# Clustered attention and two expert layers: reciprocal sums spread by transfers through device memory, additions of output halves one step later

## The chip, the cores and the metric

One program on one core of a Trainium2 chip. The metric is the device time of one execution in microseconds (us), the median over runs. Five engines run in parallel, each in the order of its own instructions: PE (TensorE, matrix products, with its weight loads shown apart as PEld), DVE (VectorE), ACT (ScalarE), POOL (GpSimd) and SP (SyncE), which here issues every transfer. An instruction that needs another engine's result, or a landed transfer, waits for a semaphore at the head of its engine's queue, and everything behind it waits too.

## The reference

Attention over 2 batches, 8 heads, 768 tokens, head width 64, with 16 centroids per head. A query sees only the keys that have the same nearest centroid. Its output is the input of a layer with squared ReLU (512 to 2048 to 512), and that one's output the input of four weighted expert layers.

```
q_assign = argmax(q_n @ c_n)            # nearest centroid, per head
k_assign = argmax(k_n @ c_n)
scores = where(q_assign == k_assign, scale * q @ k^T, -1e9)
attn = exp(scores - rowmax)
attn = attn / (sum(attn) + 1e-9)        # <- the sums whose reciprocals are spread
x    = (attn @ v) as [1536, 512]        # heads side by side
x    = relu(x @ w_in)^2 @ w_out
out  = sum_e p[:, e] * (relu(x @ w1[e]) @ w2[e]),  p = probs / (sum + 1e-9)
```

## The kernel before

Everything is float32; for the products each operand is split into a rounded high part and a low rest (fp32r), and two or three products are added up.

**Attention** takes the first quarter of the time. There are 16 heads (batch times heads), 6 query tiles of 128 rows each, so 96 *steps*, numbered g from 0. Two heads are a *pair* of 12 steps; "step 7" below means g = 7 mod 12, counted from a pair's first step. One step works on four tiles at once: the scores of tile g+2 (`S`, line 590: two products over 128 rows, then two over 80 rows, of which 64 are low parts of q or k and 16 the one-hot rows of the centroid mask), the exponential of tile g+1 (`E`, ACT), the transposes of tile g (`T0`, `T1`, PE, with the copy `pth` on ACT and the rest `ptl` on DVE), and half of the product with v for the pair of tiles before (`P0` or `P1`). `M` is DVE's row maximum for `S`.

The order in which a step's instructions are written is the list `ORDER`, one for even and one for odd steps, and each engine issues in that order. For odd steps it is `S X1 E M T0 T1 Y1 H0 C P1 X2 R L0 H1 C L1 O K Y2 C`. `X1` and `X2` take the next two entries of the step's list `todo`, `Y1` and `Y2` run what these return (their evacuation); entries that are left run after the last letter. `R` runs preparations (`stack`, `hot_rows`, loads), `O` is `emit_PO`, `K` a piece of the conversion of the next layer's first weights (line 189 on ACT and 191 on POOL are its last piece, in step 7 of four pairs), `C` takes one entry of `dq`, a list of small DVE and POOL steps. All four kinds of side work share one PSUM buffer, `ps_m`.

**The one-hot** of the next pair's first head runs beside: maxima on DVE and steps on POOL (lines 456 to 464), then in step 7 `pair_hot` as second entry of `todo`: PE transposes (478), ACT copies to `ohm` (483), and `hot_rows` has SP issue four transfers into the rows 64 to 79 of q2 and k2 (495). The first reader of these rows is `S` of step 10.

**emit_PO** evacuates a finished output of 256 queries. A head's product has a high and a low half in the two halves of the 128 partitions, which must be added. After the pair's first head, at `O` of step 7, SP issues `xm<-xs` (line 666), which moves the low half to the other partitions in the tile xm, of which there is **one buffer** (`bufs=1`); after the second head, at `O` of step 1 of the next pair, two more transfers complete xs and xm (669, 670). At that same `O` the list `nq` gets the eight entries of `norm_slots`, and from step 2 on each step takes one entry of `nq` and appends it to its `todo`.

**norm_slots** is the *norm chain* of a pair; there are seven in the loop (0 to 6; chain 6 falls in the last pair, which prepares no further one-hot and uses no xm), and an eighth after the loop with `last=True`. Step 2, f1: reciprocals of the sums (128 rows x 12) on DVE, split in high and low. Step 6, f2: PE transposes the 24 columns (689), ACT copies them to rt, POOL adds xs and xm in two halves (698). Steps 8 and 9, f3: three products each with the constant selector `sel` (706) spread the 6 rows of each head over its 64 partitions, ACT copies to rb (712), POOL multiplies (713) and splits into the next layer's input (726). Nothing needs that input before the attention ends.

**After the attention** come the squared-ReLU layer and the experts; the change does not touch them.

Of the kernel before, what the change touches and what calls it, by code (L numbers as in the profile page):

```python
# [8 lines left out]
F32 = mybir.dt.float32  # L9
# [3 lines left out]
ALU = mybir.AluOpType  # L13
# [20 lines left out]
def moe_attention_kernel(  # L34
# [171 lines left out]
    with tc.manual_schedule():  # L206
# [7 lines left out]
        pt_p = right(actx, "pt", 2)  # L214
        xs_p = right(actx, "xs", 2)
        sm_p = right(actx, "sm", 4)
        prep = ExitStack()
        nat_p = right(prep, "nat", 1)
        kq_p = right(prep, "kq", 1)
# [32 lines left out]

        def load_direct(i, nm):
            b, h = divmod(i, H)
            x = p_p.tile([128, NTT, D], F32, tag="p", name="p") if i == 0 else (
                xs_p.tile([128, NTT, D], F32, tag="rb", name="rb"))
            a = k if nm == "nk" else q
            nc.sync.dma_start(out=x, in_=a[b, h].rearrange("(p t) d -> p t d", t=NTT))
            nat[i, nm, "raw"] = x
# [409 lines left out]
                    nc.sync.dma_start(out=xs_t[hp][low], in_=xo[low])  # L669
                    nc.sync.dma_start(out=xm_t[hp][low], in_=xo[top])  # L670

        def norm_slots(hp, last=False):
            st = {}
            def f1():
                sm = sums_t.pop(hp)
                r = sm_p.tile([128, 2, NTT], F32, tag="r", name="r", bufs=1)
                rs = st["rs"] = sm_p.tile([128, NTT, 2, 2], F32R, tag="rs", name="rs", bufs=2)
                rv = r.rearrange("p h t -> p t h")
                dq[:0] = [
                    lambda: nc.vector.tensor_scalar(r, sm, 1e-9, None, op0=ALU.add),  # L680
                    lambda: nc.vector.reciprocal(r, r),
                    lambda: nc.vector.tensor_copy(rs[:, :, :, 0], rv),
                    lambda: (nc.vector if last else nc.gpsimd).tensor_tensor(
                        rs[:, :, :, 1], rv, rs[:, :, :, 0].bitcast(F32), op=ALU.subtract),
                ]

            def f2():
                m = ps_m.tile([NTT * 4, 128], F32R, tag="m", name="m")
                nc.tensor.transpose(m, st["rs"].rearrange("p t h s -> p (t h s)"), identr)

                def evac():
                    rt = st["rt"] = xs_p.tile([NTT * 4, 128], F32R, tag="rt", name="rt")
                    nc.scalar.copy(rt, m.bitcast(F32))
                    if hp in xm_t:
                        xm = xm_t.pop(hp)
                        for c0 in range(0, S, HALF):
                            cs = slice(c0, c0 + HALF)
                            nc.gpsimd.tensor_tensor(  # L698
                                xs_t[hp][:, cs], xs_t[hp][:, cs], xm[:, cs], op=ALU.add)
                return evac  # L700

            def f3(half):
                b, kt = divmod(hp, H // 2)
                m = ps_m.tile([128, HALF], F32, tag="m", name="m")
                for j in range(QT):
                    nc.tensor.matmul(  # L706
                        m[:, j * 128:(j + 1) * 128], sel[:, half * QT + j], st["rt"],
                        start=True, stop=True)

                def evac():  # L710
                    rb = xs_p.tile([128, HALF], F32, tag="rb", name="rb")
                    nc.scalar.copy(rb, m)
                    (nc.vector if last else nc.gpsimd).tensor_tensor(
                        rb, rb, xs_t[hp][:, half * HALF:(half + 1) * HALF], op=ALU.mult)
                    c0 = b * S + half * HALF
                    col = c0
                    while col < c0 + HALF:
                        tb, o = divmod(col, TB)
                        n = min(TB - o, c0 + HALF - col)
                        xn = rb[:, col - c0:col - c0 + n]  # L720
                        hi = xh[tb][:, kt, o:o + n]
                        if last:
                            nc.scalar.copy(hi, xn)
                        else:
                            round_pool(hi, xn)
                        (nc.vector if last else nc.gpsimd).tensor_tensor(
                            xl[tb][:, kt, o:o + n], xn, hi.bitcast(F32), op=ALU.subtract)
                        col += n
                return evac

            if last:
                return [f1, f2, lambda: f3(0), lambda: f3(1)]
            return [f1, None, None, None, f2, None, lambda: f3(0), lambda: f3(1)]


        mp = {}
# [368 lines left out]
        for g in range(NU):  # L1105
            par = g % 2
            todo = slots.pop(g, [])
            if nq:
                f = nq.pop(0)
                if f is not None:  # L1110
                    todo.append(f)
            pr, w = divmod(g - 2, 2)
            has_pv = 0 <= pr < NU // 2
            end = {}

            def slot(n):
                if todo:
                    end[n] = todo.pop(0)()

            def T(half):  # L1120
                if g < NU:
                    end["H%d" % half], end["L%d" % half] = emit_T(g, half)

            def PV(half):
                if has_pv and w == half:
                    emit_PV(pr, half)

            def PO():
                if has_pv and w == 1:
                    emit_PO(pr)  # L1130
                    ii, jj = divmod(pr, NTT // 2)
                    if ii % 2 == 1 and jj == NTT // 2 - 1 and pr + 1 < NU // 2:
                        nq.extend(norm_slots(ii // 2))

            def other():
                for f in early.pop(g, []):
                    f()

            def convert():
                if g >= AT["conv"] and cq:  # L1140
                    if not dq and g % (2 * NTT) in AT["turns"]:
                        cq.pop(0)()
                elif not cq and g % NTT == 4:
                    for _ in range(2):
                        lq and lq.pop(0)()

            def finish(n):
                f = end.pop(n, None)
                if f:
                    f()  # L1150

            def products():
                emit_S(g + 2)
                if g == NU - 1:
                    late.append(early_gemm1(0))

            def maximum():
                while late and g < NU - 1:
                    late.pop(0)()
                emit_max(g + 2)  # L1160

            do = {
                "E": lambda: emit_exp(g + 1), "S": products,
                "M": maximum, "P0": lambda: PV(0), "P1": lambda: PV(1),
                "O": PO, "R": other, "T0": lambda: T(0), "T1": lambda: T(1),
                "X1": lambda: slot("Y1"), "X2": lambda: slot("Y2"),
                "C": lambda: dq and dq.pop(0)(),
                "K": convert,
            }
            for a in ORDER[par]:  # L1170
                do[a]() if a in do else finish(a)
            while todo:
                whole(todo.pop(0))
            while late and g == NU - 1:
                late.pop(0)()
            if g == NU - 2:
                prep.close()
                mctx = ExitStack()
                for nm in ("w01", "g", "tp"):
                    mp[nm] = mctx.enter_context(  # L1180
                        tc.tile_pool(name=nm, bufs=1, reuse_waits="tile"))
                w_pool[0, 1] = mp["w01"]
                ga = mp["g"].tile([128, 12 * TB], F32R, name="ga")
                mp["g1"] = ga.rearrange("p (k x t) -> p k x t", k=6, x=2)
                mp["g2"] = ga.rearrange("p (k t) -> p k t", t=HALF)
                fa = mp["tp"].tile([128, 6 * HALF + 1024], F32, name="fa")
                mp["r"] = fa[:, 0:2 * TB].rearrange("p (k t) -> p k t", k=2)
                mp["c"] = fa[:, 0:6 * HALF].rearrange("p (k t) -> p k t", k=6)
                sa = fa[:, 6 * HALF:6 * HALF + 1024]
                mp["s"] = sa.rearrange("p (s k f) -> p s k f", s=4, k=2)  # L1190
                cv_p.append(lambda shp: sa[:, 0:512] if len(shp) == 2 else
                            sa[:, 0:512].rearrange("p (k f) -> p k f", k=shp[1]))


        hp, pr = NH // 2 - 1, NU // 2 - 1
        f1, f2, f3, f4 = norm_slots(hp, last=True)
        f1()
        while dq:
            dq.pop(0)()
# [149 lines left out]
```

## Time and profile before

| | |
|---|---|
| time, median of 3 runs | 1033.24 us (1032.88 to 1033.82) |
| the profiled execution | 1032.07 us, its span 1030.2 us |
| PE busy in the span | 1019.0 us, 99% |
| DVE, ACT, POOL busy | 675.2, 536.3, 568.2 us |
| attention, steps 0 to 95 | up to about 262 us of the span |

The page gives busy times and a chain of waits, followed back from the last instruction: at each step to what released it, or to the instruction before it on its engine. What lies on that chain sets the end. A timeline row is: start, duration of the group, engine, line, operation, tile written <- tiles read, shapes, count, and in brackets how long the engine was idle just before and what ended that. In the chain a piece's duration counts only the time until the next piece takes over, so pipelined products show 0.11 to 0.18 us each there and about 0.3 us in the timeline. SP's queue (SPq) is in the timeline too, with the time that each issue takes.

### The profile page before, as it was taken

What the parts mean: (1) busy time and instruction counts of PE and PEld (TensorE: products, weight loads), DVE (VectorE), ACT (ScalarE), POOL (GpSimd) and SP (SyncE); (2) the same over time, 40 slices, a digit from 0 to 9 for tenths busy, and PEclk for the clock granted to TensorE, in tenths of its full rate; (3) what the DMA queues carried; (4) which work ended last, traced back from release to release, by engine and by line L of the source; (5) the groups of instructions that cost most, each with busy time, mean ns of one, the idle gap of its engine ahead of it and who ended that gap; (6) DMA issues with size and microseconds to landing.
All of it is one profiled execution on the core that took longest, in us unless ns stands there. A gap on an engine that the chain in (4) does not pass through costs nothing.

```text
span 1030.2 us, 14964 instructions
## 1 busy us (share of the span) xinstructions
PE 1019.0 (99%) x5549; PEld 906.1 (88%) x5549; DVE 675.2 (66%) x1054; ACT 536.3 (52%) x1080; POOL 568.2 (55%) x564
## 2 busy tenths in 40 slices
PE   8999999999999999999999999999999999999998
PEld 7999999999888888888888889899888898988887
DVE  8888888889676773731275565577676565555554
ACT  6888889889565433434453333433354333333331
POOL 4567778663332222244456667667678566566550
PEclk9999999999999999999999999999999999999999
DMA  4676656751032320311012112122124122122101
GB/s 120 160 187 143 137 125 162 193 132 46 12 113 84 121 82 13 111 41 41 1 42 82 60 63 82 47 77 82 42 82 143 41 82 81 42 82 68 56 1 61
DMA packets 72456, 86.05 MB, mean 84 GB/s; under 512 B 26944, under 2 KB 49792, under 8 KB 72384
## 3 DMA queue, kind: packets, MB, share of 16 engines
q1 hardware_dynamic: 72384, 85.11, 28.7%
q8 instruction: 43, 0.70, 0.3%
q14 instruction: 29, 0.24, 0.1%
HBM read 59.83 MB, written 3.15 MB: 61 GB/s over the span
## 4 chain that ended last, share of the span: by engine, by line
PE 89%; DVE 5%; POOL 5%; issue 1%; ACT 1%; POOLq 0%; DVEq 0%; ACTq 0%
PE bank L920 25%; PE bank L880 22%; PE bank L773 13%; PE s L590 4%; PE t L623 4%; PE bank L750 4%; PE bank L748 4%; PE bank L749 4%; PE po L637 2%; PE po L639 2%; POOL xs L698 1%; DVE ptl L629 1%; DVE nb L599 1%; PE m L361 1%; PE m L706 1%
## 5 line engine op out<-in xcount | busy, mean ns | idle before, releaser
L920 PE MATMUL bank<-w1h,ga 128*128 128x512 f32 x768 | 269.9, 393 | 0.0
L930 DVE SCALAR_TENSOR_TENSOR x<-bank,pe_p,x 128x512 f32<-128x512 f32 x180 | 134.8, 750 | 167.8 <-PE bank L920 167.7
L880 PE MATMUL bank<-xa,w0h 128*128 128x384 f32 x896 | 228.2, 335 | 0.1
L880 PEld LDWEIGHTS bank<-xa,w0h 128*128 128x128 f32 x896 | 164.5, 188 | 17.9 <-ACT fa L891 0.5
L920 PEld LDWEIGHTS bank<-w1h,ga 128*128 128x128 f32 x768 | 144.1, 188 | 24.5
L759 POOL TENSOR_TENSOR ga<-fa,ga 128x512 fp32r<-128x512 f32 x48 | 63.2, 1317 | 175.4 <-ACT ga L758 134.4
L920 PE MATMUL bank<-w1l,ga 128*128 128x512 f32 x384 | 151.6, 395 | 0.0
L880 PE MATMUL bank<-xa,w0l 128*128 128x384 f32 x448 | 149.7, 334 | 0.0
L891 ACT COPY fa<-bank 128x384 f32<-128x384 f32 x96 | 45.6, 475 | 171.6 <-PE bank L880 171.6
L773 PE MATMUL bank<-ga,w1h 128*128 128x512 f32 x384 | 126.6, 389 | 0.0
L900 ACT ACTIVATE ga<-fa 128x384 fp32r<-128x384 f32 x96 | 50.5, 526 | 135.5 <-DVE fa L894 135.5
L849 POOL TENSOR_TENSOR w0l<-raw,w0h 128x512 fp32r<-128x512 f32 x64 | 75.0, 1194 | 81.2 <-ACT w0h L848 81.2
L867 POOL TENSOR_TENSOR w1l<-raw,w1h 128x1024 fp32r<-128x1024 f32 x32 | 77.3, 2414 | 71.3 <-ACT w1h L866 71.3
L629 DVE TENSOR_TENSOR ptl<-t,pth 128x384 fp32r<-128x384 f32 x192 | 97.9, 549 | 28.3 <-ACT pth L628 27.9
L599 DVE TENSOR_REDUCE nb<-s 128x1 f32<-128x768 f32 x96 | 91.4, 952 | 8.9 <-PE s L590 7.7
L903 DVE SCALAR_TENSOR_TENSOR ga<-fa,ga 128x384 fp32r<-128x384 f32 x96 | 90.1, 939 | 0.6 <-ACT ga L900 0.6
L628 ACT CAST pth<-t 128x384 fp32r<-128x384 f32 x192 | 83.6, 485 | 11.5 <-PE t L623 10.4
L623 PE MATMUL t<-identf,p 128*128 128x128 f32 x576 | 86.9, 275 | 1.6 <-DVE ptl L629 1.5
L610 ACT ACTIVATE p<-s,nb 128x768 f32<-128x768 f32 x96 | 87.5, 911 | 2.0 <-DVE nb L599 1.9
L756 ACT ACTIVATE fa<-bank 128x512 f32<-128x512 f32 x44 | 26.4, 599 | 116.3 <-PE bank L750 116.3
L773 PEld LDWEIGHTS bank<-ga,w1h 128*128 128x128 f32 x384 | 72.1, 188 | 14.7
L590 PE MATMUL s<-k,q 80*128 80x384 f32 (+1 forms) x384 | 84.4, 341 | 0.2 <-DVE q L334 0.2
(209 smaller groups left out, 2066.6 us busy)
## 6 DMA issues: line engine op xcount, KB each, us to landing
raw<-in_moe_w_dram SPq DMA_DIRECT2D x64, 512.0 KB, 4.1
raw<-in_moe_w_in_dram SPq DMA_DIRECT2D x7, 1024.0 KB, 5.1
raw<-in_moe_w_out_dram SPq DMA_DIRECT2D x6, 1024.0 KB, 4.9
k<-nkh SPq DMA_DIRECT2D x28, 192.0 KB, 3.3
q<-nqh SPq DMA_DIRECT2D x28, 192.0 KB, 3.0
nv<-in_v_dram SPq DMA_DIRECT2D x16, 192.0 KB, 3.9
out_dram<-x SPq DMA_DIRECT2D x12, 256.0 KB, 2.1
k<-nkl SPq DMA_DIRECT2D x14, 192.0 KB, 3.8
```

Source lines behind the costliest of these rows:

```text
L590: nc.tensor.matmul(s[:, j, 0:HALF], stk[i, nq][:, t * 128:(t + 1) * 128], stk[i, nk][:, j * HALF:(j + 1) * HALF], start=first, stop=not first)
L599: nc.vector.tensor_reduce(out=nb, in_=s_ps[u][:, :, 0:HALF], axis=AX.XY, op=ALU.max, negate=True)
L610: nc.scalar.activation(p, s_ps.pop(u)[:, :, 0:HALF], AF.Exp, bias=nb_t.pop(u), accum_out=sums_t[hp][:, i % 2, t:t + 1])
L623: nc.tensor.transpose(tp[:, j], p_sb[u][:, half, j * 128:(j + 1) * 128], identf)
L628: return (lambda: nc.scalar.copy(dh, tp), lambda: nc.vector.tensor_tensor(dl, tp, dh.bitcast(F32), op=ALU.subtract))
L629: lambda: nc.vector.tensor_tensor(dl, tp, dh.bitcast(F32), op=ALU.subtract))
L773: nc.tensor.matmul(o, a, b, start=(ft == 0 and z == 0), stop=(ft == NF - 1 and z == 2))
L867: nc.gpsimd.tensor_tensor(lo, w, hi.bitcast(F32), op=ALU.subtract)
L880: nc.tensor.matmul(ps, w[:, o:o + 128], r_op(r, x)[:, kt], start=(first and kt == 0 and z == 0), stop=(kt == 1 and z == 2), skip_group_che ...
L903: nc.vector.scalar_tensor_tensor(out=g_t(n, f, t, 1), in0=h_src(n, f, t), scalar=0.0, in1=g_t(n, f, t, 0).bitcast(F32), op0=ALU.max, op1=A ...
L920: nc.tensor.matmul(o, a, w[:, f], start=(f == 0 and z == 0), stop=(f == 1 and z == 2))
L930: nc.vector.scalar_tensor_tensor(out=acc, in0=o, scalar=pc, in1=acc, op0=ALU.mult, op1=ALU.add)
```

## The change

The norm chain inside the loop becomes `norm_steps`. The reciprocals are no longer split; PE transposes their 12 columns in step 5 instead of 6, ACT copies them, and SP writes the 12 rows of 128 to a tile in device memory. In step 6 SP issues two transfers that read 768 values back into each of 64 partitions (192 KB each). The addition of xs and xm is an entry of its own in step 7, one step later than before: there it is the third entry of `todo`, behind pair_hot, and so runs after the step's last letter (in chain 6 it is the first). Steps 8 and 9 multiply and split on POOL as before, as plain entries. rb is one tile of 768 columns for the whole attention instead of two rotating halves. After the loop `norm_last` does what `norm_slots(last=True)` did, selector products included.

```diff
+        hbm_p = actx.enter_context(tc.tile_pool(name="hbm", bufs=2, space=bass.MemoryType.DRAM))
+        rb_all = xs_p.tile([128, S], F32, tag="rb", name="rb", bufs=1)
...
-        def norm_slots(hp, last=False):
+        def norm_scaled(hp, half, rb, v, hi_copy):
+            b, kt = divmod(hp, H // 2)
+            v.tensor_tensor(rb, rb, xs_t[hp][:, half * HALF:(half + 1) * HALF], op=ALU.mult)
...
+        def norm_steps(hp):
             st = {}
+
+            def f1():
+                sm = sums_t.pop(hp)
+                r = st["r"] = sm_p.tile([128, 2, NTT], F32, tag="r", name="r", bufs=1)
+                dq[:0] = [
+                    lambda: nc.vector.tensor_scalar(r, sm, 1e-9, None, op0=ALU.add),
+                    lambda: nc.vector.reciprocal(r, r),
+                ]
+
+            def f2():
+                m = ps_m.tile([2 * NTT, 128], F32, tag="m", name="m")
+                nc.tensor.transpose(m, st["r"].rearrange("p h t -> p (h t)"), identf)
+
+                def evac():
+                    rt = xs_p.tile([2 * NTT, 128], F32, tag="rt", name="rt")
+                    nc.scalar.copy(rt, m)
+                    rd = st["rd"] = hbm_p.tile([2 * NTT, 128], F32, tag="rd", name="rd")
+                    nc.sync.dma_start(out=rd, in_=rt)
+                return evac
+
+            def f3():
+                rb = st["rb"] = rb_all[:]
+                for h in range(2):
+                    nc.sync.dma_start(
+                        out=rb[h * D:(h + 1) * D],
+                        in_=st["rd"][h * NTT:(h + 1) * NTT].rearrange(
+                            "t n -> (t n)").partition_broadcast(D))
+
+            def f4():
+                xm = xm_t.pop(hp)
+                for c0 in range(0, S, HALF):
+                    cs = slice(c0, c0 + HALF)
+                    nc.gpsimd.tensor_tensor(
+                        xs_t[hp][:, cs], xs_t[hp][:, cs], xm[:, cs], op=ALU.add)
+
+            def f5(half):
+                norm_scaled(hp, half, st["rb"][:, half * HALF:(half + 1) * HALF], nc.gpsimd, round_pool)
+
+            return [f1, None, None, f2, f3, f4, lambda: f5(0), lambda: f5(1)]
+
+        def norm_last(hp):
...
-                    if hp in xm_t:
-                        xm = xm_t.pop(hp)
-                        for c0 in range(0, S, HALF):
-                            cs = slice(c0, c0 + HALF)
-                            nc.gpsimd.tensor_tensor(
-                                xs_t[hp][:, cs], xs_t[hp][:, cs], xm[:, cs], op=ALU.add)
...
-            return [f1, None, None, None, f2, None, lambda: f3(0), lambda: f3(1)]
+            return [f1, f2, lambda: f3(0), lambda: f3(1)]
...
-                        nq.extend(norm_slots(ii // 2))
+                        nq.extend(norm_steps(ii // 2))
```

## Rows read from the trace of the kernel before

**Rows 1.** The page, busy time of the engines.
```profile
PE 1019.0 (99%) x5549; PEld 906.1 (88%) x5549; DVE 675.2 (66%) x1054; ACT 536.3 (52%) x1080; POOL 568.2 (55%) x564
```

**Rows 2.** Windows: busy us (instructions) of PE, PEld, DVE, ACT, POOL; granted clock; DMA; GB/s.
```profile
60.00:260.00 200.00, 196.24 (x1465) 184.32 (x1464) 171.66 (x300) 175.92 (x418) 133.31 (x187) 1.00 0.58 136
```

**Rows 3.** Chain of waits, steps 6 to 10 of chain 2: start, us, what.
```profile
128.16 1.94 POOL xs L698 x2
...
132.05 0.36 POOL oh L464
...
132.46 0.45 PE m L478 x3
132.91 0.78 PE s L590 x4
133.68 0.33 PE t L623 x3
134.01 0.47 PE m L706 x3
134.49 0.48 PE t L623 x3
...
136.38 0.48 PE m L706 x3
136.86 0.80 PE t L623 x6
...
138.38 0.70 PE s L590 x4
```

**Rows 4.** Timeline of PE: transposes of step 5, one-hot transposes of step 7.
```profile
126.16 0.92 PE L623 MATMUL t<-identf,p 128*128 128x128 f32 x6 [0.26 <-DVE ptl L629]
...
132.46 0.45 PE L478 MATMUL m<-identr,oh 128*128 128x128 f32 x3 [0.45 <-POOL oh L464]
```

**Rows 5.** Timeline of SP's queue, chain 2, and last the loads of chain 4.
```profile
125.94 1.34 SPq L243 DMA_DIRECT2D nq<-in_q_dram  x2
...
132.48 0.46 SPq L666 DMA_DIRECT2D xm<-xs  x1
133.45 0.66 SPq L495 DMA_DIRECT2D q<-ohm  x1
134.16 1.28 SPq L495 DMA_DIRECT2D k<-ohm  x2
...
190.97 1.11 SPq L109 DMA_DIRECT2D raw<-in_moe_w_out_dram  x2
```

**Rows 6.** Line 495, the 56 one-hot row transfers.
```profile
DMA to landing us min/median/max: 1.9/2.0/4.2
```

**Rows 7.** Timeline of DVE: the cast of chain 2, the second maximum.
```profile
123.45 0.16 DVE L682 CAST rs<-r 128x12 fp32r<-128x12 f32 x1
...
128.20 0.55 DVE L467 TENSOR_REDUCE mx<-A 128x24 f32<-128x384 f32 x1
```

**Rows 8.** Line 191 on POOL: ns min/median/max, first and last start.
```profile
L191 POOL TENSOR_TENSOR w0l<-cva,w0h x4: 1274/1276/1280, 70.4 to 164.2; 128x512 fp32r<-128x512 f32 x4
```

**Rows 9.** Timeline of POOL: the conversion in step 7.
```profile
133.02 1.27 POOL L191 TENSOR_TENSOR w0l<-cva,w0h 128x512 fp32r<-128x512 f32 x1 [0.61 <-ACT w0h L189]
```

**Rows 10.** Timeline of ACT: the conversion in step 7.
```profile
132.31 0.62 ACT L189 CAST w0h<-cva 128x512 fp32r<-128x512 f32 x1
```

**Rows 11.** Chain of waits: step 10 of chain 4, step 9 of chain 6.
```profile
200.46 0.70 PE s L590 x4
...
255.68 0.49 PE m L706 x3
...
256.25 0.48 ACT rb L712
```

**Rows 12.** DMA issues: count, KB each, median us to landing.
```profile
nq<-in_q_dram SPq DMA_DIRECT2D x12, 192.0 KB, 4.8
```

**Rows 13.** Line 976, the warm-up products at the start: ns min/median/max.
```profile
L976 PE MATMUL po<-identr x41: 278/283/583, 2.0 to 16.7; 128*128 128x256 f32 x41
```

More of the change, by code (lines that the diff above doesn't have):

```diff
@@ L254, in load_direct @@
             b, h = divmod(i, H)
+            o = 0 if nm == "nk" else HALF
             x = p_p.tile([128, NTT, D], F32, tag="p", name="p") if i == 0 else (
-                xs_p.tile([128, NTT, D], F32, tag="rb", name="rb"))
+                rb_all[:, o:o + HALF].rearrange("p (t d) -> p t d", t=NTT))
             a = k if nm == "nk" else q
@@ L670, in emit_PO @@
                     nc.sync.dma_start(out=xm_t[hp][low], in_=xo[top])
-        def norm_slots(hp, last=False):
+        def norm_scaled(hp, half, rb, v, hi_copy):
+            b, kt = divmod(hp, H // 2)
+            v.tensor_tensor(rb, rb, xs_t[hp][:, half * HALF:(half + 1) * HALF], op=ALU.mult)
+            c0 = b * S + half * HALF
+            col = c0
+            while col < c0 + HALF:
+                tb, o = divmod(col, TB)
+                n = min(TB - o, c0 + HALF - col)
+                xn = rb[:, col - c0:col - c0 + n]
+                hi = xh[tb][:, kt, o:o + n]
+                hi_copy(hi, xn)
+                v.tensor_tensor(xl[tb][:, kt, o:o + n], xn, hi.bitcast(F32), op=ALU.subtract)
+                col += n
@@ new lines, in norm_steps @@
+        def norm_steps(hp):
+            st = {}
+            def f1():
[30 more added lines that the diff above has]
+            return [f1, None, None, f2, f3, f4, lambda: f5(0), lambda: f5(1)]
@@ L678, in f1 @@
                 rv = r.rearrange("p h t -> p t h")
[L679 to L685, printed above, removed]
+                V = nc.vector
+                V.tensor_scalar(r, sm, 1e-9, None, op0=ALU.add)
+                V.reciprocal(r, r)
+                V.tensor_copy(rs[:, :, :, 0], rv)
+                V.tensor_tensor(rs[:, :, :, 1], rv, rs[:, :, :, 0].bitcast(F32), op=ALU.subtract)
             def f2():
@@ L693, in evac @@
                     nc.scalar.copy(rt, m.bitcast(F32))
-                    if hp in xm_t:
-                        xm = xm_t.pop(hp)
-                        for c0 in range(0, S, HALF):
-                            cs = slice(c0, c0 + HALF)
-                            nc.gpsimd.tensor_tensor(
-                                xs_t[hp][:, cs], xs_t[hp][:, cs], xm[:, cs], op=ALU.add)
                 return evac
             def f3(half):
-                b, kt = divmod(hp, H // 2)
                 m = ps_m.tile([128, HALF], F32, tag="m", name="m")
@@ L710, in evac @@
                 def evac():
-                    rb = xs_p.tile([128, HALF], F32, tag="rb", name="rb")
+                    rb = rb_all[:, half * HALF:(half + 1) * HALF]
                     nc.scalar.copy(rb, m)
[L713 to L728, printed above, removed]
-                return evac
-            if last:
-                return [f1, f2, lambda: f3(0), lambda: f3(1)]
-            return [f1, None, None, None, f2, None, lambda: f3(0), lambda: f3(1)]
+                    norm_scaled(hp, half, rb, nc.vector, nc.scalar.copy)
+                return evac
+            return [f1, f2, lambda: f3(0), lambda: f3(1)]
         mp = {}
@@ L1195, in moe_attention_kernel @@
         hp, pr = NH // 2 - 1, NU // 2 - 1
-        f1, f2, f3, f4 = norm_slots(hp, last=True)
+        f1, f2, f3, f4 = norm_last(hp)
         f1()
```

## The prediction

> **What bounds the kernel now.** I read the page's busy shares first: TensorE (PE) is busy for 99% of the span [rows 1]. The change touches the attention only, so next comes that stage alone: from 60 to 260 us PE is busy 196.2 of 200 us, ScalarE (ACT) 175.9, VectorE (DVE) 171.7, GpSimd (POOL) 133.3, at a granted clock of 1.00, the upper level of 2.4 GHz [rows 2]. An edit there pays or costs what it does to PE's order of work, unless a wait takes its place.
>
> Third, the chain of waits through one stretch of a head pair (chain 2 of the seven norm chains; the others repeat it). It runs on POOL: the two additions of output halves (1.94 us), the last steps of the one-hot, then PE's one-hot transposes at 132.46 [rows 3]. PE had stood idle 0.45 us for them [rows 4]. From there the chain is PE without a gap: the scores of step 8, selector products, scores of step 9, selector products, scores of step 10 at 138.38. So the selector products lie on the path, and the additions reach it by 0.45 us.
>
> Fourth, SP's queue, which no share on the page shows. At 132.48 it issues xm<-xs, at 133.45 to 135.5 the four one-hot row transfers [rows 5]. The second k<-ohm starts at 134.16 + 0.64 = 134.80 and lands 2.0 after its start [rows 6], at 136.8. Its reader is the second half of the scores of step 10 (80 rows: 64 of q or k and the 16 of the one-hot), at 138.38 + 0.35 = 138.73. The rows have 1.9 us to spare; my forecast turns on that figure.
>
> **The change part by part.** *Selector products.* Out go 0.47 and 0.48 us of products, and the transposes behind each return from 0.48 to 0.33 and from 0.80 to 0.66 [rows 3]: 0.47 + 0.48 + 0.15 + 0.14 = 1.24 us of PE per chain, in seven chains (the eighth, at the end, keeps its products). ACT's two copies of rb (0.48 each) go too; in chains 0 to 5 they lie beside PE's work and give nothing more.
>
> *The transpose of the reciprocals, one step earlier.* It costs about a third of a selector group, 0.16 us. In step 5 PE waits 0.26 us for DVE before its transposes [rows 4], and that hides it; without that cover it would cost the same 0.16 as before and gain nothing. Step 6 loses it: 0.16 off. The cast of the reciprocals on DVE goes as well (0.16 [rows 7]), and a small subtraction on POOL that nothing waits for any more. The cast stands three steps before the one-hot in DVE's unbroken order, so it is worth between nothing and 0.16 per chain; I take nothing, because PE has other work by then.
>
> *The additions, one step later: what they free.* The one-hot's second half on POOL needs DVE's maximum, ready at 128.20 + 0.55 = 128.75 [rows 7], where it now starts after the additions at 130.10. So it ends 1.35 us earlier and PE's idle 0.45 goes; next late is PE itself.
>
> *The same move: what it holds.* xm has one buffer. The addition reads the old xm; the next pair's xm<-xs writes it, in step 7. Today the additions are over two us before that transfer. Now they are written into the program at the very end of step 7, behind the transfer and behind the weight conversion of that step. So SP must wait for POOL at xm<-xs, and behind it on SP stand the four one-hot rows. In chains 0 to 3 (the conversion's subtraction runs on POOL four times, 70.4 to 164.2 [rows 8]) the times are, if everything up to step 7 stays:
> - conversion on POOL 133.02 + 1.27 = 134.29 [rows 9]; it can't start sooner, because it waits for ACT's w0h (132.31 + 0.62 = 132.93) [rows 10], which follows step 7's own copies;
> - additions 1.94: 136.23;
> - xm<-xs, then the rows, at the gaps of [rows 5] (0.46 for itself, here 0.5, 0.71 for the first row, 0.64 for the next): the second k<-ohm starts at 138.1, lands at 140.1, with 0.1 for two hand-overs (132.41 to 132.46 is one) 140.2.
>
> PE would want it at 138.73 - 1.24 - 0.45 - 0.16 = 136.9, stands idle for 3.3 us, and goes on at 140.2 - 0.16 = 140.04 instead of 138.73: **+1.3 us in each of four chains**, though 1.85 us of PE work and idling were taken out of each. The landing of such rows was 1.9 at best and 4.2 at worst [rows 6], so one chain costs between +1.2 and +3.5; I take the median. PE does not win it back: the steps that follow are PE without a gap.
>
> In chains 4 and 5 no conversion is left. The additions end near 128.75 + 2.31 (the one-hot's second half, 130.10 to 132.41) + 1.94 = 133.0 in the same coordinates, 0.5 after today's issue of xm<-xs, so the rows land some 0.5 later, 137.3, and PE wants them at 138.73 - 1.40 = 137.3: even. Chain 5 gains the 1.40. Chain 4 is held by SP for another reason: two weight loads end at 190.97 + 1.11 = 192.08 [rows 5]; behind them the new write to device memory, for whose landing the two broadcasts must wait on SP (2.0 from its start, as the one-hot rows, the smallest transfers here; 194.1), the broadcasts (0.55 each, between xm<-xs and a row; 195.2), two stack transfers (0.6 each; 196.4), xm<-xs and the rows: the second k<-ohm starts at 198.25 and lands at 200.25, with a hand-over 200.3, where PE read it at 200.46 + 0.35 = 200.81 [rows 11]. Chain 4 gains 0.5.
>
> Chain 6 has no one-hot and no xm behind it. Its products go (0.49 in the second group), and there ACT's rb copy does lie on the path (0.48) [rows 11]. The first group's 0.63 and at least as much of the second: -1.2.
>
> *The transfers themselves.* SP is free after the q loads, 125.94 + 1.34 = 127.3 [rows 5]. The write has landed by 129.3, the second broadcast (192 KB each) starts at 129.85. No broadcast stands in the trace; the nearest row, loads of that size from device memory, takes 4.8 [rows 12], so 134.7 (the fastest landing of any row, 1.9, gives 131.8). POOL gets to the multiplication after the additions, at 136.2: hidden, with 1.5 to spare. If that cover is gone, POOL waits, and behind it stand the splits of v and of the next k and q; that is a rival below.
>
> *Sum.* 4 x 1.3 - 0.5 - 1.4 - 1.2 = **+2.1 us** on the profiled execution's 1032.07 (span 1030.2 and 1.9 around it); that execution is 1.2 below the median 1033.24, to which I add the sum: **1035.3 us**. A difference under 0.2% (2.1 us) is about what can't be told from no change; the forecast stands on that border.
>
> **Rivals.**
> - *The rows still come in time* (0.15). For it: today they have 1.9 to spare, and the additions depend on nothing late. Against: one buffer of xm, and the order of the program. It decides at 136.9: if the additions end by 132.9, or the xm transfer needs no wait, PE gets all it saves: 4 x 1.85 + 0.5 + 1.4 + 1.2 = 10.5 off, 1022.7.
> - *PE's clock falls in the new idle stretches* (0.11). PE stands 3.3 us four times, where the trace has gaps of 0.45 at a steady 1.00. The nearest price is the first warm-up products: 583 ns at the slowest, 278 at the fastest [rows 13], so twice as long. If 1.5 to 3 us of work run at half rate after each gap, that is 6 to 12 more: 1041.3 to 1047.3. The Trainium skill ("TensorE: Matmul & The Clock Gate", section "HAM oscillation — how this bites in real kernels") speaks against this change: waits between groups of products let the engine be throttled to half its clock, again and again; no row of this trace shows such a gap, so it stays a rival.
> - *The broadcasts or the write land late* (0.11). All 64 destination rows read one source row, for which there is no row. If the write takes 4.2 instead of 2.0, SP is late by 2.2 in chains 4 and 5 (chains 0 to 3 wait longer for POOL anyway): about 3.5 more, 1038.8. A broadcast some 3 us late moves POOL's splits, not PE, at first.
>
> **How the numbers follow.** My forecast gets 0.63, with its own range 1033 to 1039 (landing times, and how much of the 1.24 per chain ACT and DVE let PE keep). The unknowns (landings, hand-overs, a broadcast for which there is no row) lean to the long side, so it puts 0.32 past 1035.3, 0.30 within 0.2% and 0.01 below. Slower: 0.32 + 0.11 + 0.08 = 0.51; the same: 0.30 + 0.03 = 0.33; faster: 0.15 + 0.01 = 0.16. The range 1029.5 to 1042 holds the forecast, the third rival and the cheap end of the second, and leaves out the first and most of the second, 2 in 10.
>
> **What would show it.** Right: in SP's queue xm<-xs waits for POOL's addition in chains 0 to 5, and the one-hot rows are issued some 3 us later in the first four; PE's scores of step 10 stand idle for a transfer, about 3 us four times and little in the other two; no idle before the one-hot transposes; two steps 1.24 shorter in PE's busy time; PE about 9 us less busy over the stage, which is as long or longer. Wrong: xm<-xs is issued as early as today, the scores of step 10 follow without a gap, and the stage is about 10 us shorter; or PE's idle stands at the multiplication's side, behind POOL waiting for rb; or the granted clock leaves 1.00.

## Result and profile after

The changed kernel takes 1047.98 us (median of 4 runs, 1047.67 to 1048.58), the kernel before 1033.06 us beside it (1032.76 to 1033.82): ratio 1.0144, 95% interval 1.0126 to 1.0162. That is slower, by 14.9 us where 2.1 were forecast, and outside the range. The profiled execution has a span of 1045.8 us, 15.6 more than before.

The page, as for [rows 1]; below it the granted clock of PE in 40 slices, and the group of the scores' products with the idle time before them and what ended most of it:

```profile
PE 1020.0 (98%) x5507; PEld 907.0 (87%) x5507; DVE 676.4 (65%) x1047; ACT 531.9 (51%) x1066; POOL 567.9 (54%) x557
...
PEclk9999989999999999999999999999999999999999
...
L593 PE MATMUL s<-k,q 80*128 80x384 f32 (+1 forms) x384 | 88.7, 351 | 17.1 <-DMA k<-ohm 13.8
```

PE has 42 instructions fewer and is busy 1.0 us *longer*: something makes the rest slower. The page's clock row shows a single 8, so the clock has to be read in narrow stretches. And 17.1 us of idle time stand in one group. Line 593 is line 590 of before; here are its waits, in the timeline of PE:

```profile
78.49 0.59 PE L593 MATMUL s<-k,q 80*128 80x384 f32 x2 [3.22 <-DMA q<-ohm]
...
111.46 0.98 PE L593 MATMUL s<-k,q 80*128 80x384 f32 x2 [3.04 <-DMA k<-ohm]
...
145.86 0.98 PE L593 MATMUL s<-k,q 80*128 80x384 f32 x2 [3.01 <-DMA k<-ohm]
...
181.68 0.59 PE L593 MATMUL s<-k,q 80*128 80x384 f32 x2 [2.98 <-DMA k<-ohm]
...
216.21 0.59 PE L593 MATMUL s<-k,q 80*128 80x384 f32 x2 [3.56 <-DMA k<-ohm]
...
248.37 0.59 PE L593 MATMUL s<-k,q 80*128 80x384 f32 x2 [1.17 <-DMA k<-ohm]
```

One wait for one-hot rows in each of chains 0 to 5. Twice the same pair of products takes 0.98 instead of 0.59 us. The windows (columns as in [rows 2]) say why, for the whole stage and for the stretch behind the wait of chain 2:

```profile
60.00:260.00 200.00, 182.71 (x1312) 172.18 (x1312) 159.07 (x271) 156.97 (x371) 125.34 (x170) 0.96 0.63 149
...
145.00:146.00 1.00, 0.14 (x1) 0.17 (x2) 0.00 (x0) 0.00 (x0) 0.91 (x2) 0.65 0.23 49
145.30:145.60 0.30, 0.00 (x0) 0.00 (x0) 0.00 (x0) 0.00 (x0) 0.30 (x1) 0.50 0.03 7
146.00:152.00 6.00, 6.00 (x26) 5.81 (x27) 2.95 (x5) 2.14 (x5) 4.10 (x8) 0.50 0.77 175
152.00:153.00 1.00, 1.00 (x10) 1.00 (x9) 0.34 (x2) 0.94 (x3) 0.98 (x2) 0.94 0.23 47
```

For some 6.2 us after the wait PE is busy without a break at a granted clock of 0.50, the lower level of 1.2 GHz. Each microsecond of work at 0.50 loses half a microsecond: half of the 0.14 before 146, 6 x 0.50 and 0.06 make 3.1 us in chain 2. Read the same way, the stretch behind the wait of chain 1 loses 1.6 and those of chains 3 and 4 lose 1.7 each; behind those of chains 0 and 5 the clock stays at 1.00. Together 8.1 us. In chains 1 and 2 the clock is down already while PE still waits (the row from 145.30), which costs nothing; the figures of 3.4 and 8.5 in the expectations below count that idle time as lost too.

Why the rows come late shows in SP's queue, chain 2 (compare [rows 5]):

```profile
131.58 1.34 SPq L245 DMA_DIRECT2D nq<-in_q_dram  x2
133.02 0.99 SPq L708 DMA_DIRECT2D rd<-rt  x1
136.45 1.13 SPq L714 DMA_DIRECT2D rb<-rd  x2
...
141.82 0.46 SPq L669 DMA_DIRECT2D xm<-xs  x1
142.38 0.66 SPq L498 DMA_DIRECT2D q<-ohm  x1
143.09 1.28 SPq L498 DMA_DIRECT2D k<-ohm  x2
```

and beside it in the timeline of POOL:

```profile
138.57 1.28 POOL L191 TENSOR_TENSOR w0l<-cva,w0h 128x512 fp32r<-128x512 f32 x1 [1.58 <-ACT w0h L189]
139.81 1.98 POOL L723 TENSOR_TENSOR xs<-xs,xm 128x384 f32<-128x384 f32 x2
141.74 1.21 POOL L677 TENSOR_TENSOR rb<-rb,xs 128x384 f32<-128x384 f32 x1
```

The additions end at 141.79, and xm<-xs is issued at 141.82: SP waited for POOL, with the one-hot rows queued behind. It waited at a second place too: from the write's issue (133.02) to that of the two reads that depend on it (136.45) 3.4 us pass. The waits of SP give both sums (what SP waited for: us, times, longest):

```profile
SPq L714 <- DMA rd<-rt: 16.8, 7, 3.6
...
SPq L669 <- POOL xs L723: 9.8, 5, 2.9
```

**Where the 15.6 us are.** The second half of the scores of step 10 starts in chains 0 to 5 later than before by 2.3, 3.9, 7.1, 11.7, 15.4 and 16.9 us (before: 76.15, 107.52, 138.73, 169.94, 200.81, 231.5). Of the first figure 0.6 was there ahead of chain 0; the first one-hot transposes, at 39.95 before, start between 39.5 and 40.7 in the profiled runs below, of either form, so I count that to no step. What one chain adds to the figure of the chain before, less the clock's loss between them: +1.7, +1.6, +1.6, +1.5 in chains 0 to 3, +1.95 in chain 4, -0.25 in chain 5, and -1.3 from there to the end. With 8.1 for the clock and the 0.6 that is 15.5. Being differences of one row they must add up; that the clock's part has the right size is for an experiment to show.

### The profile page after: what moved, and what is told of

The parts are those of the page before. It is cut to its first block, busy times and chain, and to the rows that moved or that the text cites. A ratio compares the mean times of both kernels' runs of the same rounds, so it can differ in the third digit from the quotient of the medians.

```text
span 1045.8 us, 14874 instructions
## 1 busy us (share of the span) xinstructions
PE 1020.0 (98%) x5507; PEld 907.0 (87%) x5507; DVE 676.4 (65%) x1047; ACT 531.9 (51%) x1066; POOL 567.9 (54%) x557
## 4 chain that ended last, share of the span: by engine, by line
PE 90%; DVE 5%; DMA 2%; ACT 1%; issue 1%; POOL 1%; SPq 0%; ACTq 0%; DVEq 0%; POOLq 0%
PE bank L954 25%; PE bank L914 22%; PE bank L807 13%; PE t L626 5%; PE s L593 5%; PE bank L784 4%; PE bank L783 4%; PE bank L782 4%; PE po L640 3%; PE po L642 3%; DVE ptl L632 1%; DMA k<-ohm 1%; PE m L364 1%; DVE nb L602 1%; PE m L414 1%
## 5 line engine op out<-in xcount | busy, mean ns | idle before, releaser
L593 PE MATMUL s<-k,q 80*128 80x384 f32 (+1 forms) x384 | 88.7, 351 | 17.1 <-DMA k<-ohm 13.8
```

The lines of the kernel that those rows point to most:

```text
L593: nc.tensor.matmul(s[:, j, 0:HALF], stk[i, nq][:, t * 128:(t + 1) * 128], stk[i, nk][:, j * HALF:(j + 1) * HALF], start=first, stop=not first)
```

## Experiments

Theory: the late additions hold xm, the write to device memory holds SP a second time, and PE's waits for the rows drop its clock. Rivals: the transfers themselves cost, or only one of the waits matters. Ratios are against the kernel before on the same chip.

**Additions back in step 6.**

```diff
-            return [f1, None, None, f2, f3, f4, lambda: f5(0), lambda: f5(1)]
+            return [f1, None, None, f2, f34, None, lambda: f5(0), lambda: f5(1)]   # f34: f4, then f3
```

> The changed kernel with only the additions moved back into step 6, ahead of the one-hot's second half; transfers through device memory stay. Theory A (xm<-xs waits in SP's queue for the late additions and holds the one-hot rows, PE idles about 3 us in five pairs, and its clock falls to half after most of these gaps): both losses go, PE keeps some 1.24 us per chain, the 0.45 idle before the one-hot transposes returns in four chains: 1024 to 1029, granted clock 1.00 throughout; a remaining gap at most in chain 4, where SP waits for the write. Rival B (the transfers themselves cost the time: SP held by the write's landing, loads and broadcasts in each other's way): still above 1038.

Measured: 1035.63 us, ratio 1.0023 (1.0006 to 1.0040); runs from 1032.2 to 1040.1. 12 us are regained, but not the saving: the time lies between the two theories. SP no longer waits for POOL, but PE's timeline still shows waits for the rows, which now come with the write alone, in chains 0 and 4 for instance:

```profile
77.04 0.59 PE L593 MATMUL s<-k,q 80*128 80x384 f32 x2 [1.73 <-DMA k<-ohm]
...
206.00 0.59 PE L593 MATMUL s<-k,q 80*128 80x384 f32 x2 [2.48 <-DMA k<-ohm]
```

**The late additions alone**, in the kernel before, its selector products kept.

```diff
-                    if hp in xm_t:
-                        xm = xm_t.pop(hp)
...
-            return [f1, None, None, None, f2, None, lambda: f3(0), lambda: f3(1)]
+            return [f1, None, None, None, f2, adds, lambda: f3(0), lambda: f3(1)]
```

> The kernel before with only the additions one step later; selector products stay, no transfer through device memory. Theory A: the rows land as late as in the changed kernel, 1.5 us after PE wants them today, in chains 0 to 3: +6, about 1039; PE's gaps are about 1.9 us, and if its clock falls after these too, another 1.7 each, up to 1046. Rival B: no transfers, so no loss: 1032 to 1034.

Measured: 1043.25 us, ratio 1.0097 (1.0082 to 1.0112): the move alone makes 10.0 of the 14.9 us. Its waits, in the timeline of PE (line 590 here):

```profile
77.51 0.60 PE L590 MATMUL s<-k,q 80*128 80x384 f32 x2 [2.17 <-DMA k<-ohm]
...
110.68 0.72 PE L590 MATMUL s<-k,q 80*128 80x384 f32 x2 [2.12 <-DMA k<-ohm]
```

2.1 to 2.5 instead of 3.0 us in chains 0 to 3: PE still has the 0.95 of selector products to do meanwhile. Chains 4 and 5 have none. So the wait of chain 4 comes with the transfers; that of chain 5 needs the transfers and the move, since the additions back in step 6 also leave none there.

**Idle products for PE in the waits**: 24 products of 256 columns (8 in the last chain) between the two halves of the scores of step 10; their result is not used.

```diff
+                if not first and u % (2 * NTT) == 0 and u >= 4 * NTT:
+                    for _ in range(8 if u == 14 * NTT else 24):
+                        nc.tensor.matmul(w[:, 0:256]...)
```

> The changed kernel, but between the first and second half of the scores of step 10 PE runs idle products (24 of 256 columns in chains 0 to 4, 8 in chain 5, about 2.9 and 1 us) whose result nobody reads, so that it has no long gap. Theory A: the rows land as late as before, but the clock stays at 1.00; the time at half clock, by the windows 1.7 + 3.4 + 1.7 + 1.7 = 8.5 us of loss, comes back: 1038 to 1041. Rival C (the clock's dip falls into time that PE would have waited anyway): 1046 to 1049.

Measured: 1039.43 us, ratio 1.0058 (1.0041 to 1.0074). The clock was read in a second run of the same kernel:

> The same kernel as in the run with idle products between the halves of the scores, for a profile of its granted clock. Theory A (8.5 us of the loss are the halved clock behind the gaps): the clock is 1.00 in all stretches while the sync queue's waits stay as long as in the changed kernel; about 1039 us. Rival (the products only take the gaps' place and the clock is not the cause): the clock is still 0.50 behind the gaps, about 1048 us.

Measured: 1039.45 us. The stage in the windows, and SP's wait for the write:

```profile
60.00:260.00 200.00, 198.19 (x1500) 188.14 (x1498) 166.82 (x283) 163.74 (x389) 127.29 (x172) 1.00 0.63 150
```

```profile
SPq L721 <- DMA rd<-rt: 16.4, 7, 3.8
```

The waits on SP are nearly as they were (16.4 us for the write where it had 16.8, 8.0 for POOL's additions where it had 9.8), the clock is 1.00 throughout, and 1047.98 - 1039.45 = 8.5 us are gone (8.9 with each time taken against the kernel before beside it): about the 8.1 read from the windows. This is the clock's share, shown.

**xm<-xs behind the one-hot rows**, issued in step 9.

```diff
-                    xm_t[hp] = xs_p.tile(...)
-                    nc.sync.dma_start(out=xm_t[hp][top], in_=xs_t[hp][low])
+                    at(early, 2 * pr + 5, move)   # move: the two lines above
```

> The changed kernel with only xm<-xs issued two steps later, in step 9, so that the one-hot rows stand ahead of it in SP's queue; the additions stay late. Theory A: no gap of 3 us in chains 0 to 3, the clock stays at 1.00, PE keeps 1.24 + 0.45 + 0.16 per chain: 1023 to 1027, with what is left of a gap in chain 4, where SP waits for the write's landing. Rival B: above 1038.

Measured: 1033.04 us, ratio 0.9998 (0.9981 to 1.0015), runs from 1029.7 to 1036.6. The 15 us are back, the saving isn't: expected too low. PE's waits are down to 1.0 to 1.2 us in chains 0 to 2, but not in chain 4:

```profile
76.17 0.58 PE L593 MATMUL s<-k,q 80*128 80x384 f32 x2 [1.20 <-DMA k<-ohm]
...
202.49 0.65 PE L593 MATMUL s<-k,q 80*128 80x384 f32 x2 [3.88 <-DMA k<-ohm]
```

There, in SP's queue, 4.9 us lie between the write and the reads that need it, and the rows stand behind these:

```profile
190.96 0.34 SPq L710 DMA_DIRECT2D rd<-rt  x1
195.85 1.14 SPq L716 DMA_DIRECT2D rb<-rd  x2
...
198.37 0.66 SPq L498 DMA_DIRECT2D q<-ohm  x1
```

**The reads behind the additions**, at the end of step 7, the multiplications one step later; alone, and together with the edit above.

```diff
-            return [f1, None, None, f2, f3, f4, lambda: f5(0), lambda: f5(1)]
+            return [f1, None, None, f2, None, f43, None, lambda: f5(0), lambda: f5(1)]   # f43: f4, then f3
```

> The changed kernel with the load of xm left where it is, but the two broadcasts of the reciprocals moved from ahead of the additions in step 7 to behind them, at the end of the step, and the multiplications one step later. Theory A (the single buffer of xm makes the sync queue wait ahead of the one-hot rows in chains 0 to 3, the write's landing does so in chains 4 to 6): the waits of 3.0 us stay in chains 0 to 3 with the halved clock behind them, the wait of 3.56 us in chain 4 goes; 1041 to 1043 us against 1048.0. Rival B (the write's landing is what makes the one-hot rows late everywhere, and xm only fills the rest of the same time): the gaps shrink to 1.5 us or less in all chains, the clock stays at 1.00, 1035 us or less.

> The changed kernel with both things put behind the one-hot rows on the sync queue: the load of xm in step 9 and the broadcasts at the end of step 7 behind the additions. Theory A (these two waits, and the clock that falls behind them, are the whole loss): TensorE has no gap over 1.2 us ahead of the second half of the scores of step 10, the granted clock is 1.00 throughout, and the saving of the removed products shows: 1022.5 to 1025 us, faster than either kernel. Rival B (something else of the change costs time as well, such as the later additions holding TensorE's result banks or VectorE's later order): 1031 us or more at a clock of 1.00.

Measured: 1074.42 us, ratio 1.0393 (1.0376 to 1.0410), and 1055.42 us, ratio 1.0214 (1.0199 to 1.0229). Both theories missed in both. The waits for the rows went as theory A has it (3.0 us left in chains 0 to 3 of the first, at most 0.72 in the second), but a new one came. The waits of POOL in the first:

```profile
POOL rb L677 <- DMA rb<-rd: 55.2, 7, 9.7
```

and PE's timeline in the second:

```profile
162.31 0.69 PE L414 MATMUL m<-nqh,cp 128*128 128x384 f32 x1 [2.70 <-POOL nqh L52]
```

The reads land after POOL has come to the multiplications; it waits, and behind it in its queue stand the splits of the next k and q, for which PE then waits 2.7 us a chain (clock 0.89 in that window of 30 us). The broadcasts were hidden in the change only because they were early.

**The write on ACT's queue**, alone, and together with the moved xm<-xs.

```diff
-                    nc.sync.dma_start(out=rd, in_=rt)
+                    nc.scalar.dma_start(out=rd, in_=rt)
```

> The changed kernel with one edit: the write of the reciprocals is issued from ScalarE's queue; the load of xm stays ahead of the one-hot rows on the sync queue. Theory A (the single buffer of xm holds the rows in chains 0 to 3, the write holds them in chain 4): TensorE's gaps of 3.0 us and the half clock behind them stay in chains 1 to 3, chain 4's gap goes; 1043 to 1045 us. Rival B (the write ahead of everything on the sync queue is the larger cause): the gaps shrink to about 1 us everywhere, 1036 us or less.

Measured: 1043.39 us, ratio 1.0102 (1.0088 to 1.0115), as theory A has it, except that chain 4 still waits 2.43 us, and that the clock falls to 0.50 behind chain 0's wait too. The wait for xm comes forward in the waits of SP, 16.1 us where it had 9.8 behind the write's:

```profile
SPq L669 <- POOL xs L723: 16.1, 6, 3.8
```

```profile
216.41 0.58 PE L593 MATMUL s<-k,q 80*128 80x384 f32 x2 [2.43 <-DMA k<-ohm]
```

> The changed kernel with the load of xm in step 9 and the write of the reciprocals issued from ScalarE's queue instead of SyncE's; the broadcasts stay on the sync queue ahead of the one-hot rows and wait for the write. Theory C (the write lands late because it stands behind the loads that the sync queue issued before it): the write's issue to the broadcasts' issue shrinks from 2.3 to 4.9 us to about 2 us, and the time is 1026 to 1030 us. Rival D (the landing is the write's own time, whichever queue issues it): 3 us or more again, and about 1033 us as with the load of xm moved alone.

Measured: 1028.68 us, ratio 0.9953 (0.9938 to 0.9968), faster than either kernel; clock 1.00 in all windows, and only one wait over 0.35 us ahead of the second half of those scores (0.66). The write takes 2.4 to 3.6 us in chains 0 to 5, about as rival D says (only chain 4's is much shorter, 3.1 instead of 4.9); the time is theory C's. What ACT's queue saves is mainly the turn: the write goes out 0.3 us after ACT's copy starts, while SP is still issuing loads. The timelines of ACT and of SP in chain 2:

```profile
126.95 0.26 ACT L708 COPY rt<-m 12x128 f32<-12x128 f32 x1
127.24 0.30 ACTq L710 DMA_DIRECT2D rd<-rt  x1
```

```profile
126.59 1.73 SPq L245 DMA_DIRECT2D nq<-in_q_dram  x2
130.59 1.13 SPq L716 DMA_DIRECT2D rb<-rd  x2
```

Still, chains 0 to 3 take 31.3 us each (one-hot transposes at 70.14, 101.48, 132.81, 164.10), as before (69.89, 101.24, 132.46, 163.66 there): PE's 1.24 us are not seen. DVE is busy 28.33 of the 30 us from 120 to 150 (before 26.77). In its timeline (chain 2) the weight conversions are long:

```profile
136.52 0.96 DVE L167 TENSOR_SCALAR cva<-raw 128x512 int32<-128x512 int32 x1
...
139.19 1.12 DVE L170 TENSOR_SCALAR cva<-cva 128x512 f32<-128x512 f32 x1
```

Before they took 0.62 and 0.42. Here POOL works through them without a pause: a subtraction of 1.00 us from 139.03 ends at 140.03, about where a conversion of 0.42 that ends at 140.31 would start. The Trainium skill ("SBUF — State Buffer", section "SBUF: two separate sides") has it that VectorE in its fast modes and GpSimd share a port under an exclusive lock, so that the later one waits for the other's instruction to end; the rows agree within 0.15 us.

**GpSimd's instructions in halves**, in that kernel.

```diff
-                for c0 in range(0, S, HALF):
+                for c0 in range(0, S, HALF // 2):   # so for the multiplications and subtractions too
```

> The kernel with the load of xm in step 9 and the write on ScalarE's queue (1028.7 us, no gap on TensorE over 0.7 us), with GpSimd's additions, multiplications, their subtractions and v's subtraction cut into halves: twice the instructions, half as long each, the same arithmetic. Theory P (in chains 0 to 3 the rest of the saving is lost on VectorE, whose weight conversions take 0.95 to 1.33 us instead of 0.42 to 0.68 because each waits for the GpSimd instruction under way to end): the conversions of lines 167, 170 and 178 shrink by 0.3 us or more each, some 0.5 us a chain come back, 1026 to 1027.5 us. Rival Q (the conversions' length is set otherwise, or is off the path): 1028 us or more, with lines 167, 170 and 178 as long as before.

Measured: 1031.33 us, ratio 0.9978 (0.9969 to 0.9987), slower than without the cut. The conversions of theory P shrank, line 167 by a little less than it said (DVE's timeline: 0.70, 0.75, and line 178 0.92 instead of 1.33); line 173, which it doesn't name, grew from 0.41 to 0.70 in two of three chains:

```profile
136.58 0.70 DVE L167 TENSOR_SCALAR cva<-raw 128x512 int32<-128x512 int32 x1
...
139.00 0.75 DVE L170 TENSOR_SCALAR cva<-cva 128x512 f32<-128x512 f32 x1
```

But each cut costs POOL (the additions 2.46 instead of 1.97 us), and PE waits for it at the end of its run of work:

```profile
150.69 0.45 PE L417 MATMUL m<-nql,cp 128*128 128x384 f32 x1 [0.58 <-POOL nql L376]
```

Shorter GpSimd instructions, though no less work in all, gave shorter conversions: that fits conversions which wait for the instruction under way. That this is what keeps the 1.24 us is not shown, since POOL became late in its place.

**The transfers without the move**: additions back in step 6, the write on ACT's queue (both edits as above).

> The transfers of the reciprocals without the move: the changed kernel with the additions back in step 6, where they were before, and the write issued from ScalarE's queue; the load of xm stays in step 7. Theory A (the late additions make the wait for xm, and SyncE's turn makes the write late; without both the transfers pay): no gap over 1 us ahead of the second half of the scores of step 10, the 0.45 us ahead of the one-hot transposes is back, clock 1.00; 1024 to 1028 us, the fastest of all. Rival B (the write's landing still holds the rows, or POOL waits for the broadcasts when it reaches the multiplications earlier): gaps over 1 us at the scores or on POOL's side, 1031 us or more.

Measured: 1026.28 us, ratio 0.9939 (0.9925 to 0.9952), the lowest time of all, though the interval overlaps that of the 1028.68 above; theory A. The timeline of PE has the waits it expected, and one of 1.25:

```profile
100.41 0.45 PE L481 MATMUL m<-identr,oh 128*128 128x128 f32 x3 [0.54 <-POOL oh L467]
106.11 0.59 PE L593 MATMUL s<-k,q 80*128 80x384 f32 x2 [0.67 <-DMA k<-ohm]
...
197.15 0.59 PE L593 MATMUL s<-k,q 80*128 80x384 f32 x2 [1.25 <-DMA k<-ohm]
```

The conversions of lines 167 and 170 are back at 0.42 us (the first of line 167 takes 0.56; line 173 now 0.44 to 0.63), the clock at 1.00. By the prediction's own terms, 1.40 in each of chains 0 to 5 and 1.2 in chain 6 are 9.6 us; less the 0.67 and 1.25 above, and 0.2 ahead of the one-hot transposes in chains 4 and 5 each, 7.3. The span is 5.8 us shorter, its first one-hot 0.6 later: 6.4, so the removed products give most of what was worked out for them, and some 0.9 us are not traced.

## Why the prediction was wrong

- **Place, sign and the wait's mechanism were right.** SP waits for POOL at xm<-xs (in five of the six chains; in chain 4 the write holds SP past the additions), the rows are issued late, PE's wait was put at 3.3 us and measures 3.0, the second k<-ohm (from 143.09 + 0.64) released PE 2.1 after its start (2.0 taken). Four chains cost 6.4 us where 4 x 1.3 = 5.2 were taken. About half of that gap is a slip in the prediction: it counts the idle 3.3 from a landing at 140.2 but the 1.3 from 140.04; from one landing they are 3.3 and 1.5, or 3.1 and 1.3. Chain 6 gives 1.3 (1.2). There is no idle left ahead of the one-hot transposes.
- **The step that failed** is "PE does not win it back: the steps that follow are PE without a gap", taken as the steps of before at the speed of before. They ran at half clock for 3 to 6 us after four of the six waits: 8.1 us by the windows, 8.5 to 8.9 by the run with idle products, with no term in the sum. The trace of before held nothing on this: its waits were of 0.45 us [rows 4], so the steady 1.00 [rows 2] said nothing of waits of 3. Rival 2 had the mechanism and the price (6 to 12 us); with a forecast that itself puts PE idle for 3.3 us four times, a chance of 0.11 for it was far too low. The Trainium skill's rule cited there ("TensorE: Matmul & The Clock Gate", section "HAM oscillation — how this bites in real kernels") held in the main: this trace agrees, with 0.50 behind four waits, but not behind the other two.
- **Chains 4 and 5 were mis-sized.** The write, taken at 2.0 from the rows of [rows 6], takes 2.3 to 4.5 in chains 0 to 5, and 4.0 in chain 4 (from 204.97 to the reads at 209.01). That is rival 3: chain 4 costs 1.95 instead of giving 0.5, 2.0 of these 2.45 by the write. I took the rivals as alternatives; they came together, and on top of the forecast. Chain 5 gives 0.25 instead of 1.4, and not by the write, whose reads go out at 239.14. There xm<-xs waits for the additions (241.43 + 1.99 = 243.42), and the issue of the first row takes 1.62 us where 0.66 is usual, for a reason that stays open:

```profile
243.44 0.46 SPq L669 DMA_DIRECT2D xm<-xs  x1
244.00 1.62 SPq L498 DMA_DIRECT2D q<-ohm  x1
```

- **"The rows still come in time", 1022.7,** priced PE alone. With late additions and at most 0.66 us of such waits it is 1028.7: in chains 0 to 3 the 1.24 do not show. POOL's work beside DVE's conversions is the likely cause, not a shown one.
- **The broadcasts were hidden** from PE as said, but not from POOL, for which 1.5 us to spare were forecast: it waited for rb in 3 of 7 chains (12.5 us in all), and PE for none of that.

## What to carry to other kernels

A transfer at the head of an issuing queue that waits for another engine holds every unrelated transfer behind it: before moving the reader of a single-buffered tile, look up who writes the tile next and what is queued behind that. A forecast that leaves PE idle for some microseconds needs a term for its clock. A small write that another transfer must read back belongs on a queue which has nothing else to issue at that moment.

## What the hardware showed that I had not expected

- **The length of a wait does not tell whether the clock falls.** Behind 3.22 us (chain 0) it stayed at 1.00, behind 2.98 (chain 3) it went to 0.50; with the additions moved alone, 2.12 and 2.08 us led to a mean of 0.94 in the windows of 30 us around them, 2.17 and 2.46 to none; with the additions back in step 6 the window around a wait of 1.73 us has 0.94. Nor does the fall keep to the wait's end: in the changed kernel it came some 0.6 us before PE's products in chain 2 and 1.2 us after they began in chain 3. And executions of one kernel differ: with the additions back in step 6 the mean clock of the span lay between 0.994 and 1.000, and the times between 1032.2 and 1040.1. What else decides stays open.
- **A 6 KB write to device memory and the release of its reader** took 1.35 to 4.9 us on SP's queue and 1.3 to 3.6 on ACT's. Those of 1.3 to 1.4 came in chain 6 only, where in the changed kernel transfers moved 5 GB/s meanwhile, against 127 to 233 around the others.
